# Ten of 32 attention heads go back to the two-pass score scheme; constants joined, token-weight decoding and instruction order set anew

## The chip, the cores and the metric

The kernel runs on one core of a Trainium2 chip. A core has five engines that run their own instruction streams side by side and meet at semaphores: TensorE (PE in the profile, its weight loads PEld), VectorE (DVE), ScalarE (ACT), GpSimd (POOL) and SyncE (SP), which here only issues DMAs. Times are device microseconds of one execution, and less is better.

## What is computed

Attention in which a query sees only keys with the same 6-bit hash, over 4 batches of 8 heads with 768 tokens and 64 channels, then a block on each batch's 768 x 512 result:

```python
q_bits = einsum('bhsd,dk->bhsk', q, proj) > 0      # k likewise, proj is 64 x 6
mask = q_bucket[:, :, :, None] == k_bucket[:, :, None, :]
scores = where(mask, scale * matmul(q, k.T), -1e9)
scores = scores - max(scores, axis=-1)
attn = exp(scores); attn = attn / (sum(attn, axis=-1) + 1e-09)
x = matmul(attn, v)                                # heads side by side: 768 x 512
theta = x @ w_theta
y = w_tok_r @ (x * cos(theta)) + w_tok_i @ (x * sin(theta))
u = x + y
out = u + maximum(u @ w_ch, 0)
```

The four weights are 64-bit floats, and the kernel decodes them on the chip.

## The kernel before

Every f32 operand is held as a pair of f16 numbers, high and low, and a product is made of three f16 matmuls (high x high, high x low, low x high). So a tile of the token product `py` is 36 matmuls of 512 columns, and each of `ps_th` (theta) and `ps_r` (the channel product) is 12.

Heads come in pairs (b, hp). For each pair SP loads `raw` q and k and `vb`, ACT and DVE split them, PE makes the hash signs (`bits`, tile `pb`), and SP copies the pieces into a head's operand tiles `qt` and `kt` (`assemble`: 6 DMAs, `assbits`: 4 small ones from `rows`). There are three sets of `qt` and `kt`.

A head is then done in one of two ways.

The **two-pass way** (22 heads). `maxima` scores the head with queries on the partitions (tile `sq`, 9 units in the two PSUM banks of pool `mx`), and DVE takes the row maxima (`vmax`, `mc<-sq`). PE turns the maxima (`mtr`, tile `pmx`), DVE writes them as f16 rows (`row`, `fl`), and SP puts them into `qt` (`put`) and `ft` (`putf`). `step` then scores the head a second time with keys on the partitions (tile `st`, 9 units in pool `s`), with the maximum as one more row of the operand; ACT takes the exponential (`pf`), ACT makes its f16 high part and POOL the low part (`p1`, `p2`, tile `p`), and PE multiplies them with v (`pv`, tile `po`).

The **turned way** (10 heads, list `TURNED`: heads 5 and 7 of batch 1, and 1, 3, 5, 7 of batches 2 and 3). `turned` scores once, with queries on the partitions (tile `bt`, 12 halves of 384 keys, in pools `s` and `mx`). DVE takes the maximum of each half (`bmax`, `bm<-bt`) and three small steps make bias and rate of the exponential (`bjoin`, `brate`, `bbias`). ACT takes the exponential straight from those scores, ACT and POOL split it (tile `late`), and SP turns the 128 x 1536 f16 result by a DMA transpose (`bturn`, `late<-late`), 6 in a head, before PE multiplies with v (`bpv`).

The token weights come in six tiles (`prep_wtok`, tile number tau). Each is two loads of 768 KB, a decode on DVE and ACT (`wlow`, `whigh`, `wsign`, `wabs`, `wmul`, `wth`, `wtl`) and two DMA transposes into `wtk`. Tiles below `LATE` go through the buffers x, z0 and z1, the others through wx and wz, which the turned heads use for `late` afterwards.

The order on every engine is written out by hand: `ORDER` lists an engine letter and an operation number for each operation, `SLOTS` gives each its buffer, and `issue_all` emits just that. An engine runs its list in order, so an operation that waits holds all behind it. While a batch's heads run, PE fills in the block of the batch before. SP's DMAs share eight semaphores in turn, so each issue also waits for one that was issued earlier.

Of the kernel before, what the change touches and what calls it, by code (L numbers as in the profile page):

```python
# [11 lines left out]
F16 = mybir.dt.float16  # L12
# [20 lines left out]
def lsh_attention_moe_kernel(ctx: ExitStack, tc: tile.TileContext, q, k, v, proj, w_theta, w_tok_r, w_tok_i, w_ch, aff, out):  # L33
# [4 lines left out]
    NB = proj.shape[1]  # L38
# [21 lines left out]
    affs = const.tile([P, 2], F32, name="affs")  # L60
# [9 lines left out]
    pp = const.tile([P, NB], F32, name="pp")  # L70
# [88 lines left out]

    cload = op("consts", QKL - 0.03, on("ACT", 1800, load_consts))  # L160
    proj_ready = op("pst", QK0, on("DVE", 610, split_proj), [cload])


# [26 lines left out]
    def widened(srcs, n, nm, tag, prio, am=None, stage="x", by=1.0, scaled=None, into=None, hold=()):  # L190
# [5 lines left out]
        def load():  # L196
            t["w64"] = w64 = mp.tile([P, m, n, 2], U32, tag=sx.tag, name=f"w64_{nm}")
            for i, src in enumerate(srcs):
                dma(w64[:, i].rearrange("p n two -> p (n two)"), src)
            if into is None:  # L200
# [6 lines left out]
            w2 = w64.rearrange("p m n two -> p (m n) two")  # L207
            t["lo"], t["hi"] = w2[:, :, 0], w2[:, :, 1]

        def low():  # L210
            DVE.tensor_scalar(t["f"].bitcast(U32), t["lo"], 29, 0x40000000, ALU.logical_shift_right, ALU.bitwise_xor)
# [457 lines left out]
    def step(g, b, h, blk, mxt, vt, piece):  # L669
# [85 lines left out]
        finish(t, sm_, g + KN, b, h, vt, done, lo, hi, False)  # L755

    def finish(t, so, pr, b, h, vt, done, lo, hi, eps):
        nm = f"{b}_{h}_{lo}"
        sx = xslot[b]
        n_ = hi - lo  # L760

        def recip():
            t["rc", lo] = ap_.tile([P, T], F32, tag=f"rc{so.idx}_{lo}", bufs=1, name=f"rc_{nm}")
            if eps:
                DVE.tensor_scalar(t["rc", lo][:, lo:hi], t["acc"][:, lo:hi, D], ONE * 1e-9 * PSC, None, ALU.add)
            else:
                DVE.reciprocal(t["rc", lo][:, lo:hi], t["acc"][:, lo:hi, D])

        def again():
            DVE.reciprocal(t["rc", lo][:, lo:hi], t["rc", lo][:, lo:hi])  # L770

        def norm():
            if b not in tl:
                tl[b] = mp.tile([P, T, DM], F32, tag=sx.tag, bufs=1, name=f"x_{b}")
            dst = tl[b][:, lo:hi, h * D : (h + 1) * D]
            DVE.scalar_tensor_tensor(dst, t["acc"][:, lo:hi, :D], vt["inv"], t["rc", lo][:, lo:hi].unsqueeze(2).to_broadcast([P, n_, D]), ALU.mult, ALU.mult)

        r = op("beps" if eps else "recip", pr, on("DVE", 75 if eps else 90, recip), [done], [so])
        if eps:
            r = op("brec", pr, on("DVE", 98, again), [r], [so])  # L780
        n = op("norm", pr, on("DVE", 135 + 67 * n_, norm), [r], [so, sx])
        for i in range(lo // 2, hi // 2):
            xready[b][i].append(n)

    homes = [Slot("wx"), Slot("wz")] if TURNED else []
    late = {}
    bt = {}
    HS = S // 2
    CEXP = 1.0 / (UNIT * math.sqrt(D))

    def home(n, sl):
        if n not in late:
            late[n] = mp.tile([P, 4, S], F32, tag=homes[n].tag, name=f"late{n}")
        return late[n][:, sl.idx].bitcast(F16)

    def turned(g, b, h, blk, n_, asm, vt, pieces):

        j = h % 2
        qt, kt = qts[n_], kts[n_]
        sx = xslot[b]  # L800
        i0, ni = BLOCKS[blk]
        t = bt.setdefault((b, h), {"done": None, "so": Slot("m") if blk == 0 else None, "mc": Slot("mc") if blk == 0 else None})
        so, smc = t["so"], t["mc"]
        for i in range(i0, i0 + ni):
            def one(i=i, before=t["done"]):
                nm = f"{b}_{h}_{i}"
                sp, spt = Slot("pp"), Slot("pt")
                u = {}
                G = g + 0.45 * (i - i0)

                def part(k):
                    return t["bm"][:, i, k : k + 1]

                tops, cuts, held = [], [], []
                for y in range(2):
                    def half(y=y):
                        sw = Slot(("s", "mx")[y])
                        w = {}

                        def scores():  # L820
                            w["w"] = bank(sw, [P, HS], f"bt_{nm}_{y}")
                            for x, kk in ((0, K1), (1, MR)):
                                mm(w["w"], qt[:kk, x, ts(i, P)], kt[:kk, x, y * HS : (y + 1) * HS], x == 0, x == 1)

                        def top():
                            if "bm" not in t:
                                t["bm"] = ap_.tile([P, T, 5], F32, tag="bm" + smc.tag, bufs=1, name=f"bm_{nm}")
                            DVE.tensor_reduce(part(y), w["w"], AX.X, ALU.max)  # L828

                        a = op("bst", G, on("PE", 326, scores), asm, [sw])  # L830
# [635 lines left out]
```

## Time and profile before

| | |
|---|---|
| median of 3 runs | 738.8 us (732.48 to 740.75) |
| the profiled execution | 734.01 us, of which 732.2 us is the span of its instructions |
| PE busy | 670.3 us (92%) |
| PEld busy | 388.7 us (53%) |
| DVE busy | 572.0 us (78%) |
| ACT busy | 571.2 us (78%) |
| POOL busy | 388.7 us (53%) |
| DMA | 100.07 MB, 61.1% of the queue's 16 engines |

The shares are means over stages with different limits, so they are read stage by stage. The span is cut here at the ends of each batch's attention: batch 0 until 157 us, batch 1 until 334, batch 2 until 499, batch 3 until 653, and then the rest of the last batch's block.

### The profile page before, as it was taken

What the parts mean: (1) busy time and instruction counts of PE and PEld (TensorE: products, weight loads), DVE (VectorE), ACT (ScalarE), POOL (GpSimd) and SP (SyncE); (2) the same over time, 40 slices, a digit from 0 to 9 for tenths busy, and PEclk for the clock granted to TensorE, in tenths of its full rate; (3) what the DMA queues carried; (4) which work ended last, traced back from release to release, by engine and by line L of the source; (5) the groups of instructions that cost most, each with busy time, mean ns of one, the idle gap of its engine ahead of it and who ended that gap; (6) DMA issues with size and microseconds to landing.
All of it is one profiled execution on the core that took longest, in us unless ns stands there. A gap on an engine that the chain in (4) does not pass through costs nothing. (4 is left out here: it accounts for less than half of the span.)

```text
span 732.2 us, 16801 instructions
## 1 busy us (share of the span) xinstructions
PE 670.3 (92%) x6174; PEld 388.7 (53%) x6174; DVE 572.0 (78%) x1299; ACT 571.2 (78%) x1014; POOL 388.7 (53%) x392
## 2 busy tenths in 40 slices
PE   3698979888999999888899999989999999999997
PEld 1266747664555555555445555555555466654443
DVE  6799969889999888877898868677988768678221
ACT  6689879988997797978898778878997788966012
POOL 4164444635646675757445667767546577822002
PEclk9799989999999999999999999999999999999999
DMA  5637875686326358876835598887753586971122
GB/s 210 186 94 189 231 187 150 147 178 167 79 77 127 89 123 165 187 157 152 155 78 124 105 198 141 198 150 179 137 111 76 120 147 124 164 130 44 29 68 90
DMA packets 197434, 100.07 MB, mean 137 GB/s; under 512 B 169624, under 2 KB 187112, under 8 KB 197352
## 3 DMA queue, kind: packets, MB, share of 16 engines
q1 hardware_dynamic: 197048, 99.00, 61.1%
q8 instruction: 48, 0.79, 0.4%
q14 instruction: 34, 0.28, 0.1%
q10 hardware_dynamic: 304, 0.00, 0.0%
HBM read 32.51 MB, written 6.29 MB: 53 GB/s over the span
## 5 line engine op out<-in xcount | busy, mean ns | idle before, releaser
L717 POOL TENSOR_TENSOR p<-pf,p 128x512 f16<-128x512 f32 x162 | 196.3, 1224 | 141.3 <-ACT p L711 105.6
L77 PE MATMUL py<-z,wtk 128*128 128x512 f16 x864 | 207.7, 379 | 0.1
L624 DVE TENSOR_REDUCE mc<-sq 128x1 f32<-128x512 f32 (+1 forms) x198 | 132.2, 681 | 26.1 <-PE sq L77 24.9
L870 POOL TENSOR_TENSOR late<-pf,late 128x384 f16<-128x384 f32 x120 | 113.8, 959 | 62.6 <-ACT late L864 54.5
L705 ACT ACTIVATE pf<-st 128x512 f32<-128x512 f32 x198 | 114.2, 591 | 34.0 <-PE st L77 24.4
L77 PE MATMUL st<-qt,kt 108*128 108x512 f16 (+3 forms) x528 | 119.4, 333 | 13.0 <-ACT pf L705 6.0
L77 PEld LDWEIGHTS <-wtk 128*128 128x128 f16 x864 | 82.5, 98 | 90.8 <-issue 3.9
L711 ACT ACTIVATE p<-pf 128x512 f16<-128x512 f32 x162 | 99.3, 627 | 5.1 <-PE po L77 3.5
L77 PE MATMUL sq<-kt,qt 108*128 108x256 f16 (+1 forms) x264 | 74.9, 340 | 20.2 <-DVE mc L624 5.5
L856 ACT ACTIVATE pf<-bt,bm 128x384 f32<-128x384 f32 x120 | 77.8, 664 | 17.8 <-DVE bm L844 11.0
L77 PEld LDWEIGHTS <-p 128*128 128x128 f16 x1944 | 77.8, 98 | 17.0 <-issue 1.0
L77 PE MATMUL po<-vv,p 128*128 128x65 f16 (+1 forms) x1944 | 83.9, 194 | 0.0
L828 DVE TENSOR_REDUCE bm<-bt 128x1 f32<-128x384 f32 x120 | 63.2, 549 | 21.8 <-PE bt L77 19.5
L77 PEld LDWEIGHTS <-qt 108*128 108x128 f16 (+1 forms) x504 | 47.1, 102 | 61.3 <-issue 25.8
L77 PEld LDWEIGHTS <-kt 108*128 108x128 f16 (+1 forms) x528 | 49.8, 102 | 47.4 <-issue 25.9
L77 PE MATMUL ps_th<-wth,t_x 128*128 128x512 f16 x288 | 68.9, 379 | 4.4 <-DMA t_x<-s_x 3.7
L77 PE MATMUL ps_r<-wch,t_u 128*128 128x512 f16 x276 | 70.3, 385 | 1.2 <-DMA t_u<-s_u 1.1
L864 ACT ACTIVATE late<-pf 128x384 f16<-128x384 f32 x120 | 60.4, 520 | 2.1 <-DMA late<-late 0.6
L77 PE MATMUL bt<-kt,qt 108*128 108x384 f16 x240 | 56.3, 327 | 1.9 <-DMA kt<-rows 1.7
L77 PEld LDWEIGHTS <-t_x 128*128 128x128 f16 x288 | 27.0, 97 | 35.3 <-DMA t_x<-s_x 6.7
L77 PEld LDWEIGHTS <-late 128*128 128x128 f16 x1080 | 38.5, 98 | 9.6 <-DMA late<-late 2.4
L1101 POOL TENSOR_TENSOR z<-f,z 128x512 f16<-128x512 f32 x15 | 19.5, 1300 | 43.5 <-ACT z L1095 27.8
(179 smaller groups left out, 1042.2 us busy)
## 6 DMA issues: line engine op xcount, KB each, us to landing
raw<-in_q_dram SPq DMA_DIRECT2D x16, 384.0 KB
raw<-in_k_dram SPq DMA_DIRECT2D x16, 384.0 KB
vb<-in_v_dram SPq DMA_DIRECT2D x16, 384.0 KB
out_dram<-x SPq DMA_DIRECT2D x24, 256.0 KB
qt<-hl SPq DMA_DIRECT2D x31, 192.0 KB
kt<-hl SPq DMA_DIRECT2D x31, 192.0 KB
w_t<-in_moe_w_tok_r_dram SPq DMA_DIRECT2D x6, 768.0 KB
w_t<-in_moe_w_tok_i_dram SPq DMA_DIRECT2D x6, 768.0 KB
```

The costliest lines, as they stand in the source:

```text
L77: PE.matmul(out_, l, r, start=start, stop=stop, skip_group_check=True)
L624: DVE.tensor_reduce(col()[:, cs], u["sq"], AX.X, ALU.max)
L705: ACT.activation(wide("pf", spf, F32), u["st"], AF.Exp, scale=1.0 / (UNIT * math.sqrt(D)))
L711: ACT.activation(o_, u["pf"], AF.Copy)
L717: return lambda: eng.tensor_tensor(wide("p2", sp2, F16), u["pf"], u["p1"], ALU.subtract)
L828: DVE.tensor_reduce(part(y), w["w"], AX.X, ALU.max)
L856: ACT.activation(w["f"], w["w"], AF.Exp, bias=part(4), scale=part(3))
L864: ACT.activation(dst(0), w["f"], AF.Copy)
L870: return lambda: eng.tensor_tensor(dst(1), w["f"], dst(0), ALU.subtract)
L1101: return lambda: eng.tensor_tensor(t["z"][r, 1][:, tt], u["f"], t["z"][r, 0][:, tt], ALU.subtract)
```

## The change

- `turned` and the list `TURNED` go. All 32 heads are done the two-pass way.
- The projection and the two threshold columns come as one array that the host lays out, in one DMA in place of three. The 8 small DVE operations of `split_proj` become 2.
- `LATE` falls from 4 to 2, so four of the six token-weight tiles go through wx and wz. In `widened` the load now takes only the buffer of the raw words, and the sign step depends on `wlow` instead of on the load.
- `ORDER` and `SLOTS` are new throughout, made with later DMA landings assumed.

```diff
@@ load_consts, split_proj
-        for j in range(2):
-            ACT.dma_start(pp[j * D : (j + 1) * D, :], proj)
-        ACT.dma_start(affs, aff)
+        ACT.dma_start(pp, proj)
...
-        for nm, first in (("q", 1.0), ("k", -1.0)):
-            for j in range(2):
-                rows = slice(j * D, (j + 1) * D)
-                for n, sgn in enumerate((first, -first)):
-                    c0 = j * 2 * NB + n * NB
-                    DVE.tensor_scalar(pst[nm][rows, c0 : c0 + NB], pp[rows, :], sgn, None, ALU.mult)
+        rows, signs = pp[:, : 4 * NB], pp[:, 4 * NB : 8 * NB]
+        DVE.tensor_tensor(pst["q"][:, : 4 * NB], rows, signs, ALU.mult)
+        DVE.scalar_tensor_tensor(pst["k"][:, : 4 * NB], rows, -1.0, signs, ALU.mult, ALU.mult)
@@ widened
-        a = op("wload", prio, on("SP", [(450, P * n * 8)] * m, load), slots=[sx, sz] + hold)
+        a = op("wload", prio, on("SP", [(450, P * n * 8)] * m, load), slots=[sx])
...
-        d = op("wsign", prio, on("ACT", 130 + 470 * k_, lambda: ACT.activation(t["sg"], t["hi"].bitcast(F32), AF.Sign)), [a], [sx, sz])
+        d = op("wsign", prio, on("ACT", 130 + 470 * k_, lambda: ACT.activation(t["sg"], t["hi"].bitcast(F32), AF.Sign)), [b_], [sx, sz])
@@ the calls by head
-                if (b, 2 * hp + j) in TURNED:
-                    mxs.append((n, asm))
-                    continue
                 mxs.append(maxima(2 * hp + j, n, b, G, asm))
...
-                if (b, 2 * hp + j) in TURNED:
-                    ends = b == B - 1 and hp == NP - 1
-                    turned(g, b, 2 * hp + j, blk, *mxs[j], vt, LASTP if ends else [(0, T)])
-                    g += BLOCKS[blk][1] // 2
-                    continue
                 step(g, b, 2 * hp + j, blk, mxs[j], vt, PIECES[ORD if b == B - 1 and hp == NP - 1 else 0].get(blk))
@@ constants
-TURNED = [(1, 5), (1, 7), (2, 1), (2, 3), (2, 5), (2, 7), (3, 1), (3, 3), (3, 5), (3, 7)]
-LATE = 4
-WL0 = 22.644
-WLS = 8.829
+LATE = 2
+WL0 = 16.0
+WLS = 2.6
```

What the new numbers do is seen in the order on the engines. On SP, near the start, where the second pair's q and k (`raw_0_1`), the second token-weight tile (`w_t`) and head 1's operands (`hl` into `qt` and `kt`) are fetched, before:

```order
L455 DMA raw_0_1_225<-in_q_dram 128x768
L199 DMA w_t_227<-in_moe_w_tok_r_dram 128x1536
L199 DMA w_t_227<-in_moe_w_tok_i_dram 128x1536
L571 DMA qt_137<-hl_0_179 64x2x768
L572 DMA kt_140<-hl_0_179 64x2x768
```

and after, where head 0's maxima (`row_0`) are put as well:

```order
L456 DMA raw_0_1_229<-in_q_dram 128x768
L572 DMA qt_136<-hl_0_171 64x2x768
L573 DMA kt_139<-hl_0_171 64x2x768
L575 DMA qt_136<-hl_0_171 32x768
L576 DMA kt_139<-hl_0_171 32x768
L575 DMA qt_136<-hl_0_171 32x768
L576 DMA kt_139<-hl_0_171 32x768
L650 DMA qt_135<-row_0_272 1x6x128
```

The 1.5 MB of the second weight tile have moved from ahead of head 1's operands to behind head 1's own maxima, 23 issues later, and the put of head 0's maxima has moved ahead of the four small `rows` copies that it stood behind.

On PE, in batch 2 around the turn of head 6's maxima (`pmx_6`), with the block of batch 1 (`py`) as filling; head 7 was a turned head. Before:

```order
L638 MATMUL pmx_6_7050<-ident,mx_6_6787 6x128
L77 LDWEIGHTS qt_138
L77 MATMUL bt_7_0_0_7052<-kt_141,qt_138 128x384
L77 LDWEIGHTS qt_138
L77 MATMUL bt_7_0_0_7052<-kt_141,qt_138 128x384
L77 LDWEIGHTS wtk_101
L77 MATMUL py_4_6832<-z_1_4720,wtk_101 128x512
```

After:

```order
L639 MATMUL pmx_6_7170<-ident,mx_6_6856 6x128
L77 LDWEIGHTS qt_137
L77 MATMUL sq_7_1_7174<-kt_140,qt_137 128x512
L77 LDWEIGHTS kt_138
L77 MATMUL st_5_0_5_7180<-qt_135,kt_138 128x512
L77 LDWEIGHTS kt_138
L77 MATMUL st_5_0_5_7180<-qt_135,kt_138 128x512
L77 LDWEIGHTS qt_137
L77 MATMUL sq_7_2_7190<-kt_140,qt_137 128x256
```

Head 7 now has its first scores (`sq_7`) here, between the second scores of head 5 (`st_5`), which the turned way did not have.

## Rows read from the trace of the kernel before

**Rows 1.** Windows by stage: PE, PEld, DVE, ACT, POOL busy us (instructions), clock, DMA share, GB/s

```profile
0.00:157.00 157.00, 126.46 (x1173) 85.90 (x1174) 132.33 (x299) 127.48 (x227) 70.40 (x85) 0.95 0.65 174
157.00:334.00 177.00, 162.79 (x1610) 93.31 (x1610) 154.13 (x337) 151.09 (x280) 108.23 (x101) 0.99 0.60 137
334.00:499.00 165.00, 154.83 (x1520) 88.29 (x1522) 128.57 (x312) 137.12 (x246) 103.21 (x103) 0.99 0.71 142
499.00:653.00 154.00, 152.85 (x1536) 87.98 (x1529) 123.62 (x301) 129.90 (x229) 98.45 (x97) 1.00 0.68 132
653.00:732.20 79.20, 73.42 (x343) 33.22 (x341) 33.36 (x53) 25.61 (x35) 8.39 (x7) 0.99 0.24 60
```

**Rows 2.** The chain that ended last: start us, us, what

```profile
469.41 0.89 PE st L77 x8
...
664.67 27.84 PE py L77 x129
```

**Rows 3.** Timeline of PE at 442 us: start us, us, instructions [idle before]

```profile
442.37 0.60 PE L77 MATMUL sq<-kt,qt 108*128 108x512 f16 x3
442.81 0.90 PE L77 MATMUL po<-vv,p 128*128 128x65 f16 x24
...
444.19 0.82 PE L77 MATMUL bt<-kt,qt 108*128 108x384 f16 x4
444.86 0.81 PE L77 MATMUL ps_r<-wch,t_u 128*128 128x512 f16 x3
```

**Rows 4.** Page, costliest groups: xcount | busy, mean ns | idle before

```profile
L624 DVE TENSOR_REDUCE mc<-sq 128x1 f32<-128x512 f32 (+1 forms) x198 | 132.2, 681 | 26.1 <-PE sq L77 24.9
...
L705 ACT ACTIVATE pf<-st 128x512 f32<-128x512 f32 x198 | 114.2, 591 | 34.0 <-PE st L77 24.4
...
L711 ACT ACTIVATE p<-pf 128x512 f16<-128x512 f32 x162 | 99.3, 627 | 5.1 <-PE po L77 3.5
...
L856 ACT ACTIVATE pf<-bt,bm 128x384 f32<-128x384 f32 x120 | 77.8, 664 | 17.8 <-DVE bm L844 11.0
...
L828 DVE TENSOR_REDUCE bm<-bt 128x1 f32<-128x384 f32 x120 | 63.2, 549 | 21.8 <-PE bt L77 19.5
...
L864 ACT ACTIVATE late<-pf 128x384 f16<-128x384 f32 x120 | 60.4, 520 | 2.1 <-DMA late<-late 0.6
```

**Rows 5.** Groups by form: the small steps of turned heads, the end of a token-weight decode

```profile
L844 DVE TENSOR_SCALAR bm<-bm 128x1 f32<-128x1 f32 x60 | 12.6, 211 | 1.5
...
L300 DVE TENSOR_TENSOR wf_t<-wf_t 128x768 f16<-128x768 f32 x12 | 11.4, 963 | 0.6 <-ACT wf_t L299 0.6
...
L225 DVE SCALAR_TENSOR_TENSOR wf_t<-wf_t,scw 128x1536 f32<-128x1536 f32 x6 | 11.1, 1846 | 0.0
...
L838 DVE TENSOR_REDUCE bm<-bm 128x1 f32<-128x2 f32 x60 | 9.1, 151 | 1.5
L841 DVE TENSOR_SCALAR bm<-bm 128x1 f32<-128x1 f32 x60 | 9.1, 151 | 1.5
```

**Rows 6.** Waits of PE over the whole span: us in total, times, longest

```profile
PE st L77 <- ACT pf L705: 6.0, 8, 1.6
PE sq L77 <- DVE mc L624: 5.5, 15, 0.8
PE pmx L638 <- DVE mx L634: 4.3, 4, 1.9
...
PE st L77 <- DMA qt<-row: 3.9, 5, 2.0
...
PE sq L77 <- DMA kt<-rows: 3.6, 3, 2.2
...
PE bt L77 <- DMA kt<-rows: 1.7, 2, 1.5
PE po L77 <- DMA late<-late: 1.6, 2, 1.0
```

**Rows 7.** Timeline of PE in the first 30 us

```profile
6.00 1.49 PE L77 MATMUL pb<-raw,pst_q 128*32 128x384 f32 x2 [6.00 <-DVE pst_q L158]
...
27.43 1.01 PE L77 MATMUL sq<-kt,qt 108*128 108x512 f16 x2 [3.85 <-DMA kt<-hl]
```

More of the change, by code (lines that the diff above doesn't have):

```diff
@@ L32, in lsh_attention_moe_kernel @@
 @with_exitstack
-def lsh_attention_moe_kernel(ctx: ExitStack, tc: tile.TileContext, q, k, v, proj, w_theta, w_tok_r, w_tok_i, w_ch, aff, out):
+def lsh_attention_moe_kernel(ctx: ExitStack, tc: tile.TileContext, q, k, v, proj, w_theta, w_tok_r, w_tok_i, w_ch, out):
     nc = tc.nc
@@ L37, in lsh_attention_moe_kernel @@
     B, H, D, S = q.shape
-    NB = proj.shape[1]
+    NB = (proj.shape[1] - 2) // 8
     DM = w_theta.shape[0]
@@ L69, in lsh_attention_moe_kernel @@
     ones1 = ones[:, :33]
-    pp = const.tile([P, NB], F32, name="pp")
+    pp = const.tile([P, 8 * NB + 2], F32, name="pp")
+    affs = pp[:, 8 * NB :]
     pst = {}
@@ L199, in load, with place @@
                 dma(w64[:, i].rearrange("p n two -> p (n two)"), src)
+        def place():
             if into is None:
@@ L206, in load, with words @@
                 t["f"] = into()
-            w2 = w64.rearrange("p m n two -> p (m n) two")
+        def words():
+            w2 = t["w64"].rearrange("p m n two -> p (m n) two")
             t["lo"], t["hi"] = w2[:, :, 0], w2[:, :, 1]
         def low():
+            place()
+            words()
             DVE.tensor_scalar(t["f"].bitcast(U32), t["lo"], 29, 0x40000000, ALU.logical_shift_right, ALU.bitwise_xor)
@@ L754, in step @@
         lo, hi = 2 * piece[0], 2 * piece[1]
[L755 to L759, printed above, removed]
         n_ = hi - lo
         def recip():
[L763 to L770, printed above, removed]
+            if "rc" not in t:
+                t["rc"] = ap_.tile([P, T], F32, tag=f"rc{sm_.idx}", bufs=1, name=f"rc_{nm}")
@@ L772, in norm @@
+            DVE.reciprocal(t["rc"][:, lo:hi], t["acc"][:, lo:hi, D])
         def norm():
             if b not in tl:
-                tl[b] = mp.tile([P, T, DM], F32, tag=sx.tag, bufs=1, name=f"x_{b}")
+                tl[b] = mp.tile([P, T, DM], F32, tag=xslot[b].tag, bufs=1, name=f"x_{b}")
             dst = tl[b][:, lo:hi, h * D : (h + 1) * D]
-            DVE.scalar_tensor_tensor(dst, t["acc"][:, lo:hi, :D], vt["inv"], t["rc", lo][:, lo:hi].unsqueeze(2).to_broadcast([P, n_, D]), ALU.mult, ALU.mult)
@@ L778, in finish @@
[L778 to L782, printed above, removed]
-            xready[b][i].append(n)
[L785 to L794, printed above, removed]
@@ L901, in moe @@
+            DVE.scalar_tensor_tensor(dst, t["acc"][:, lo:hi, :D], vt["inv"], t["rc"][:, lo:hi].unsqueeze(2).to_broadcast([P, n_, D]), ALU.mult, ALU.mult)
+        r = op("recip", g + KN, on("DVE", 90, recip), [done], [sm_])
+        n = op("norm", g + KN, on("DVE", 135 + 67 * n_, norm), [r], [sm_, sx])
+        for i in range(*piece):
+            xready[b][i].append(n)
     def moe(b, G):
@@ new lines @@
+Dk9 Anj Ai3 Pi9 Phm Djp A2o Del Dk1 Pke Dkf Djq Ajr Phr Phw Pic Aid Skp Pnm Dnn Aia Dno G2p Dnp D2r D2s S1b Pk6 Pif Dnq Djs Pka Pib Ahz Dkb
+Dk7 Gjt Pkg Dkh Pkc Dkd Pk2 Dk3 Dki Pir Dnr Dns Gi0 Pkw Ai4 Dkx Aig Pky A2t S2w Gi5 Dkz Pie Pi1 Dnt Ais Pkj Piu Anw Pix Dkk Dkl Aiy Pii Dnu
+Skm A2u Dnx Ssi Aij Pih Aiv Gju Pik Dnv D1c Pio Pil Aim A1e D1d Skn Pkq Pin Aip Piq Pi6 Ssg G2v Dnz Pm8 A1f Plj D2x D2y Pl2 S1q D1g D1h A30
+Am9 Asj Sof Ama Pjv Ajw D1i D1j A1m Plo Dkr Pl6 A1k D1n Gmb S1o Alp Dl7 Dl3 Pit Piw Ash Alk D1l Di7 Di8 Pks Ple Ply Piz Alf Alg Glh Alz All
@@ L1416 @@
+D31f P30u S2zo P30v A30w D30x S30y P31g P31h P31i A31j D31k S31l
 """
@@ L1433, in _thresholds, with _laid_out @@
     return a
+def _laid_out(proj):
+    import numpy as np
+    d, n = proj.shape
+    rows, signs = np.zeros((128, 4 * n), np.float32), np.ones((128, 2, 2, n), np.float32)
+    for j in range(2):
+        for i in range(2):
+            rows[j * d : (j + 1) * d, (2 * j + i) * n : (2 * j + i + 1) * n] = proj
+    signs[:, :, 1] = -1
+    return np.concatenate([rows, signs.reshape(128, 4 * n), _thresholds(n)], axis=1)
 def kernel(**inputs):
```

392 lines of the change are left out of this document (148 added, 244 removed).

## The prediction

> **What bounds the kernel now.** The page's total says PE 92%, DVE and ACT 78%, but that is a mean over stages, so the windows come first [rows 1]. The reader is to look for the row in which one engine has no idle time left. In the first stage (batch 0, 157 us) nobody is full: PE 126.5, DVE 132.3, ACT 127.5, with 30 us of PE idle, much of it the start-up. In the second (157 to 334) PE is idle for 14.2 us of 177 and DVE (154.1) and ACT (151.1) are nearly as long. In the third (334 to 499) PE is idle for 10.2 of 165. In the fourth (499 to 653) it is idle for 1.15 of 154: there PE alone sets the time. After 653 only the last block is left, and in the chain of waits it is PE again, 129 `py` matmuls in one piece of 27.84 us [rows 2], which is 0.216 us for 512 columns, with the granted clock at 0.99. So a microsecond of PE work costs a microsecond in the fourth stage and the tail, part of one in the second and third, and little in the first. Of DVE and ACT the opposite holds.
>
> **What the change does to a head.** PE: the timeline has one 512-column unit of `sq` and one pair of 256 start at 442.37 and the next work at 442.81, so two units take 0.44 us and a head's 9 units 2.0 us [rows 3]. The second scores cost what the turned head's only scores cost: 4 `bt` matmuls take 444.86 - 444.19 = 0.67 us, 24 of them 4.0 us [rows 3]; 8 `st` matmuls of 256 take 0.89 us [rows 2], so 12 take 1.33, and 12 of 512 at 0.216 take 2.6, together 3.9. The product with v keeps its 108 matmuls. Six matmuls for `ft` and one turn of the maxima are new, at 0.04 us or so each (0.90 / 24 [rows 3]) 0.2 to 0.3. That makes **+2.2 us of PE a head**, 22 us for ten: 4.4 in batch 1 (two heads), 8.8 in batch 2, 8.8 in batch 3.
>
> DVE loses 12 x 0.549 and six times 0.151 + 0.151 + 0.211 [rows 4, 5], 6.6 + 3.1 = 9.7 us, and gets 9 x 0.681 = 6.1 [rows 4] and three small steps, some 0.6: **-3 us a head**. ACT loses 12 x (0.664 + 0.520) = 14.2 us and gets 9 x (0.591 + 0.627) = 11.0 [rows 4]: **-3.2 us a head**. POOL splits the same number of elements and is nowhere the longest engine [rows 1]; I cost it at nothing, and the engine to hide behind is PE. SP loses six transposes a head and gets three small puts. PE waited 1.6 us for turned results in the whole run, and 1.7 us for the `rows` of turned heads [rows 6], so the transposes' going is worth at most some 3 us of direct wait, and I put it into the bounds.
>
> **Stage by stage,** against the profiled execution of 734.0 us (its span of 732.2 and 1.8 around it).
>
> Batch 0. The signs now wait for one load and two DVE operations, not three loads and eight. PE stood still until 6.00 us for `pst_q` [rows 7]; the first q and k are needed too, and I take 0.8 us for it. Then PE waited 3.85 us for `kt<-hl` at 27.43 [rows 7], and SP's order had the 1.5 MB of a weight tile ahead of those copies; they are behind them now. Against this, the end of a sixth weight tile's decode (1.85 + 2 x 0.96 = 3.8 us of DVE [rows 5]) moves from the second stage into this one, and the decodes stand closer together, through one buffer: a late one would hold DVE's list, `vmax` and `norm` of batch 0 behind it. I take -1, between -5 (start-up gain alone) and +5 (decode in full, and some waiting).
>
> Batch 1. DVE, 154.1, loses 2 x 3 and the 3.8 of the decode, ACT 6.4, so both fall to about 144. PE rises from 162.8 to 167.2 and becomes the longest by far; what it waited for was mostly the two that get lighter, so I take 6 us of idle in place of 14.2, which gives 173, or **-4**. Ends: idle of 2 us, -8; all idle stays, +4.4.
>
> Batch 2. PE 154.8 + 8.8 = 163.6 of 165, DVE down by 12 and ACT by 13. What was idle goes first: with some 4.4 of the 10.2 us left (the same share as in batch 1), 168, or **+3**. Ends: no idle to speak of, -2; all of it stays, +8.8.
>
> Batch 3. There is 1.15 us to give, so **+8.8**, between +8 and +11 (waits of new `sq` units that nothing covers).
>
> Tail. The same matmuls in another order: 0, between -1 and +3 (the last tile's store is late).
>
> Sum: -1 - 4 + 3 + 8.8 + 0 = +6.8, so 734.0 + 6.8 = **741 us**. The profiled execution lies 0.6% under the median of 738.8 shown, and inside the three runs' spread of 732.5 to 740.8, so I leave the sum as it is; it is 0.3% over that median. One per cent, 7.4 us, is about what a measurement of this kernel can tell from no change. All lower ends together give -8, 726; all upper ones +32, 766.
>
> **The rivals.** *The idle time closes (faster).* A new order that allows for late landings could bring the second and third stage to what the fourth has now. For it: the list of PE's waits has many short ones for DMAs [rows 6], DVE and ACT get slack, and the fourth stage shows that 99% is possible. Against it: DVE and ACT waits are as long in that list, and an order cannot move them all. Price: -5 - 8 - 2 + 8.5 - 1 = -7.5, so 726.
>
> *PE has room (faster).* Weight loads fill only 88.0 of 154 us in the fourth stage [rows 1], and if matmul records merely overlap, new matmuls could slip in between. Then the terms follow DVE and ACT alone: -1 in batch 0, -8, -4, 0, so 721. The chain's 0.216 us for 512 columns, back to back, speaks against it: that is 2.4 columns a nanosecond, the higher clock level, one column a cycle. The Trainium skill (Perfetto Trace Analysis, Identifying the Most-Contended Engine) says to judge TensorE's headroom by the share of weight loads, not by busy matmuls; by that rule the 8.8 us of batch 3 would cost nothing. Here the row of the chain decides against the rule, since 512-column matmuls take longer than their weight load.
>
> *Two-pass heads wait more (slower).* Place: the two `mx` banks and the way from the last maximum to `st`. PE's waits on that way were 6.0 + 5.5 + 4.3 + 3.9 + 3.6 = 23.3 us for 22 heads, 1.06 a head; the turned heads' were 1.7 + 1.6 = 3.3 for 10, 0.33 a head [rows 6]. Ten more heads at 0.73 are 7 us, on top of 22 us of work with none of the old idle closed, less 1 at the start: +28, 762. It decides if PE waits over 1 us a head for `vmax`, the turned maxima and their put. Against it: these waits fall mostly where DVE was full, and DVE gets lighter.
>
> *The order buys nothing (slower).* The landings were not what PE waited for, idle stays as it is in each stage, and the 22 us come on top: +4.4 + 8.8 + 8.8 - 1 = +21, 755. For it: the fourth stage, with just as many turned heads as the third, hardly waited at all, so the third's idle may have nothing to do with them.
>
> **How the numbers follow.** The forecast, 741 with its own range of 732 to 749, has 0.38; the idle closes 0.27; room in PE 0.05; more waits 0.13; an order that buys nothing 0.17. Against 738.8, faster by over 1% is below 731.4: the two faster rivals but for the upper edge of the first, and a little of the forecast's edge, 0.31. Slower is above 746.2: the two slower rivals and the forecast's upper edge, 0.33. Within 1% is the remaining 0.36. The range leaves out most of the PE rival, the bottom of the first and the upper half of the waits: 723 to 760.
>
> **What the profile after would show.** PE's busy time up by some 22 to 30 us (a `sq` record is longer than its 0.22 us step), DVE's down by about 30, ACT's by about 32, `late` and `bt` gone, 288 rows of `mc<-sq`. If the stages hold: batch 3 longer by 8 to 9 us at 99% of PE, batch 2 longer by about 3, batch 1 shorter by about 4, the attention of batch 0 ending within 5 us of 157. The first `pb` before 5.5 us, and the wait for `kt<-hl` at 27 us short or gone. I am wrong about the size if the first stage moves by more than 5 us, which I can least read from a trace with another order; about the mechanism if batch 3 does not lengthen, or if PE's wait list shows new waits for `mc` or `qt<-row` of over 1 us a head.

## The result, and the profile after

The changed kernel takes 743.99 us, median of 20 runs (737.58 to 750.15), against 737.65 for the kernel before (20 runs, 732.48 to 744.68): a ratio of 1.0085 [1.0062, 1.0108], 6.3 us. The forecast was 741, by a sum of +6.8 on the profiled execution, and 0.3% over the median known then. The total came out; the stages behind it did not all do so.

The profiled execution took 748.39 us, with a span of 746.6. It is one of the longer runs, so a second profile of the same kernel stands beside it (`again`, below, span 740.9). Windows by stage of the kernel after, to be held against [rows 1]; the columns are the same, and the cuts lie at the last `po` of each batch (the first line of `again` stands below them):

```profile
0.00:172.00 172.00, 143.54 (x1162) 95.84 (x1163) 137.19 (x283) 130.03 (x224) 70.91 (x85) 0.90 0.63 170
172.00:344.50 172.50, 167.01 (x1641) 97.00 (x1640) 151.45 (x301) 144.68 (x265) 112.10 (x97) 0.98 0.45 105
344.50:505.50 161.00, 160.16 (x1620) 93.48 (x1617) 122.60 (x242) 129.65 (x225) 102.21 (x91) 1.00 0.39 89
505.50:666.40 160.90, 160.19 (x1603) 93.85 (x1602) 110.60 (x212) 123.38 (x212) 100.16 (x87) 1.00 0.29 60
666.40:746.60 80.20, 73.68 (x344) 33.62 (x342) 35.71 (x60) 24.90 (x34) 6.46 (x5) 1.00 0.26 65
```

```profile
0.00:166.00 166.00, 137.25 (x1159) 93.06 (x1160) 136.90 (x282) 129.44 (x224) 70.88 (x85) 0.91 0.67 175
```

| stage | before | after | again | change (after, again) | forecast |
|---|---|---|---|---|---|
| batch 0 | 157 | 172.0 | 166.0 | +15.0, +9.0 | -1 |
| batch 1 | 177 | 172.5 | 173.0 | -4.5, -4.0 | -4 |
| batch 2 | 165 | 161.0 | 161.0 | -4.0, -4.0 | +3 |
| batch 3 | 154 | 160.9 | 161.0 | +6.9, +7.0 | +8.8 |
| tail | 79.2 | 80.2 | 79.9 | +1.0, +0.7 | 0 |

The cuts of before lie up to 1.8 us behind the last `po` of a batch. Cut at that mark in all three profiles (before at 155.2, 332.6, 498.0 and 652.6), the changes are +16.5 and +11.1, -4.5 and -4.4, -4.4 and -4.9, +6.2 and +6.2, and +0.7 in the tail.

In the third stage PE is now idle for 0.84 us, in the fourth for 0.71; before it was 10.2 and 1.15. PE sets the time from 345 us on. The first stage is the odd one: its PE busy time rose by 17 us with about as many matmuls (1162 for 1173), and its granted clock fell from 0.95 to 0.90.

The page of the kernel after: the clock granted in 40 slices of 18.7 us, in tenths, and the groups that answer to [rows 4].

```profile
PEclk9999995888999999999999999999999999999999
...
L625 DVE TENSOR_REDUCE mc<-sq 128x1 f32<-128x512 f32 (+1 forms) x288 | 191.4, 683 | 56.9 <-PE sq L77 55.9
L706 ACT ACTIVATE pf<-st 128x512 f32<-128x512 f32 x288 | 167.2, 591 | 82.7 <-PE st L77 55.1
...
L712 ACT ACTIVATE p<-pf 128x512 f16<-128x512 f32 x252 | 152.9, 625 | 25.7 <-PE po L77 22.7
```

The "5" is the seventh slice, 112 to 131 us: its granted clock is 0.51, so that TensorE spent nearly all of it at the lower of its two levels (1.2 GHz, 0.5 in the granted clock). There are 288 rows of `mc<-sq`, 90 more, and the groups on `bt`, `bm` and `late` are gone. DVE and ACT wait longer for PE than before: 55.9 us ahead of `mc` for 24.9, and 55.1 ahead of `pf` for 24.4 [rows 4].

The waits of PE that answer to [rows 6]:

```profile
PE sq L77 <- DVE mc L625: 8.0, 13, 1.4
PE st L77 <- ACT pf L706: 5.8, 11, 0.9
PE pb L77 <- DMA raw<-in_q_dram: 4.3, 1, 4.3
...
PE pmx L639 <- DVE mx L635: 2.0, 2, 1.0
...
PE sq L77 <- DMA kt<-rows: 1.3, 2, 0.8
```

The waits for `qt<-row` and `late` have gone, that for `kt<-rows` fell from 3.6 to 1.3. What is left of PE's waits is mostly the way from one score to the next.

PE's timeline after, the start against [rows 7] and a unit of scores against [rows 3]:

```profile
4.28 1.46 PE L77 MATMUL pb<-raw,pst_q 128*32 128x384 f32 x2 [4.28 <-DMA raw<-in_q_dram]
...
11.88 1.01 PE L77 MATMUL sq<-kt,qt 108*128 108x512 f16 x3 [4.17 <-DVE kt L540]
...
560.63 0.38 PE L77 MATMUL sq<-kt,qt 108*128 108x512 f16 x1
560.85 0.60 PE L77 MATMUL st<-qt,kt 108*128 108x256 f16 x4
561.29 2.54 PE L77 MATMUL py<-z,wtk 128*128 128x512 f16 x11
```

The first `pb` starts at 4.28 us in place of 6.00, and there is no wait at 27 us. A unit of `sq` takes 0.22 us and four half `st` 0.44, as costed.

What happened in the first stage can be read between 118 and 129 us. The same timeline of the three engines there, PE first, then ACT, then DVE:

```profile
118.14 3.51 PE L77 MATMUL po<-vw,pf 128*128 128x65 f32 x16
...
123.46 0.60 ACT L706 ACTIVATE pf<-st 128x512 f32<-128x512 f32 x1 [2.81 <-PE st L77]
123.95 1.58 ACT L222 ACTIVATE wf_t<-w_t 128x1536 f32<-128x1536 f32 x1
126.17 0.60 ACT L706 ACTIVATE pf<-st 128x512 f32<-128x512 f32 x1 [0.64 <-PE po L77]
126.66 1.47 ACT L223 ACTIVATE wf_t<-wf_t 128x1536 f32<-128x1536 f32 x1
...
128.26 0.15 DVE L172 TENSOR_SCALAR sinv<-wsum 128x1 f32<-128x1 f32 x1 [5.21 <-ACT wf_t L223]
...
130.56 0.68 DVE L625 TENSOR_REDUCE mc<-sq 128x1 f32<-128x512 f32 x1
```

Sixteen `po` with 32-bit operands take 3.51 us. In the kernel before, sixteen like them took 1.90 at the full clock:

```profile
153.34 1.90 PE L77 MATMUL po<-vw,pf 128*128 128x65 f32 x16
```

In the kernel after, ACT waits 2.81 us for `st` matmuls that stand behind them in PE's list, and 0.64 for the next `po`. So the decode step that stands behind `pf` in ACT's list (L223) comes late, and DVE, whose next step is that tile's scale, stands idle for 5.21 us; the `mc` that PE's next scores need stands behind it in DVE's list and starts at 130.56. Here a slow PE holds the decode. That the decode holds PE in turn is a reading that these rows do not show, since PE was busy for 8.9 of the 10 us from 120 on; a place where a decode does hold PE comes with order_b0_mid below.

The clock is summed here from windows of 20 us between 100 and 180 us: 20 us times (1 - granted clock) is the full-clock time that was taken away. The loss of time is at most that, since PE is also idle in these windows. Kernel after:

```profile
100.00:120.00 20.00, 16.25 (x124) 11.84 (x116) 16.37 (x35) 11.59 (x24) 9.89 (x9) 0.72 0.82 212
120.00:140.00 20.00, 18.13 (x108) 12.40 (x108) 11.64 (x24) 14.63 (x27) 3.48 (x3) 0.68 0.51 142
140.00:160.00 20.00, 15.40 (x134) 9.76 (x134) 16.98 (x33) 15.15 (x25) 12.92 (x8) 0.74 0.88 218
160.00:180.00 20.00, 16.39 (x134) 12.58 (x132) 18.07 (x40) 16.11 (x29) 4.01 (x5) 0.93 0.42 123
```

That is 5.6 + 6.4 + 5.2 + 1.4 = 18.6 us. The kernel before has 1.00 in the last three of these windows, and in the first

```profile
100.00:120.00 20.00, 17.94 (x203) 12.67 (x204) 15.02 (x37) 16.54 (x30) 8.51 (x8) 0.84 0.62 156
```

which makes 3.2 us. The table shows the runs that bear on the first stage in these terms. dup_b23 and mix_b3 have their edits behind it, so they are one more sample each of the first stage of the kernel after and of the kernel before; decode_b is left out, since its profiled execution is 1.3% longer than its median.

| kernel | PE work added in batch 0 | full-clock time lost, 100 to 180 us | last `po` of batch 0 | ratio to the kernel before |
|---|---|---|---|---|
| before | 0 | 3.2 | 155 | 1 |
| after | 0 | 18.6 | 172 | 1.0085 [1.0062, 1.0108] |
| again | 0 | 15.8 | 166 | 1.0082 [1.0043, 1.0122] |
| dup_pairs | 5.3 | 8.6 | 164 | 1.0054 [1.0021, 1.0086] |
| dup_mid | 8 | 5.2 | 163 | 1.0109 [1.0073, 1.0145] |
| dup_b0 | 16 | 1.8 | 165 | 1.0111 [1.0029, 1.0194] |
| before_dup_b0 | 16 | 3.6 | 163 | 1.0121 [1.0068, 1.0173] |
| decode_later | 0 | 7.4 | 160 | 1.0312 [1.0233, 1.0391] |
| decode5_later | 0 | 8.6 | 164 | 1.0242 [1.0189, 1.0295] |
| order_b0 | 0 | 1.2 | 155 | 1.0020 [0.9981, 1.0059] |
| order_b0_mid | 0 | 1.8 (and 12 at 57 to 81 us) | 168 | 1.0128 [1.0079, 1.0177] |
| dup_b23 | 0 | 19.4 | 168 | 1.0506 [1.0424, 1.0588] |
| mix_b3 | 0 | 1.8 | 158 | 1.0023 [0.9983, 1.0062] |

The first stage of the kernel after thus ended at 172, 166 and 168, that of the kernel before at 155 and 158; a difference of 3 us between two profiles says little.

The loss is also larger than the stage shows. By count, the 700th matmul of the kernel after starts 7.0 us ahead of that of the kernel before (10.7 in `again`), at 102.0 for 109.0, and the 1160th 16.9 us behind it (11.5). The change's order is ahead until about 100 us, with 23 of DVE's 48 steps of token-weight decode done where the kernel before has 29, and loses 22 to 24 us after that.

### The profile page after: what moved, and what is told of

Its sections match the earlier page's. It is cut to its first block, busy times and chain, and to the rows that moved or that the text cites. A ratio compares the mean times of both kernels' runs of the same rounds, so it can differ in the third digit from the quotient of the medians.

```text
span 746.6 us, 16888 instructions
## 1 busy us (share of the span) xinstructions
PE 704.6 (94%) x6364; PEld 413.8 (55%) x6364; DVE 557.5 (75%) x1094; ACT 552.6 (74%) x958; POOL 391.8 (52%) x363
## 4 chain that ended last, share of the span: by engine, by line
PE 80%; DVE 9%; ACT 6%; DMA 2%; issue 2%; SPq 1%; POOL 0%; ACTq 0%; DVEq 0%
PE py L77 24%; PE st L77 15%; PE po L77 15%; PE ps_r L77 8%; PE ps_th L77 7%; PE sq L77 7%; DVE mc L625 3%; ACT pf L706 2%; PE pb L77 2%; ACT p L712 1%; ACT wf_t L223 1%; PE pmx L639 1%; SPq L582 1%; DVE hl L473 1%; PE pm L77 0%
## 5 line engine op out<-in xcount | busy, mean ns | idle before, releaser
L718 POOL TENSOR_TENSOR p<-pf,p 128x512 f16<-128x512 f32 x252 | 309.3, 1243 | 207.0 <-ACT p L712 138.3
L625 DVE TENSOR_REDUCE mc<-sq 128x1 f32<-128x512 f32 (+1 forms) x288 | 191.4, 683 | 56.9 <-PE sq L77 55.9
L706 ACT ACTIVATE pf<-st 128x512 f32<-128x512 f32 x288 | 167.2, 591 | 82.7 <-PE st L77 55.1
L77 PE MATMUL st<-qt,kt 98*128 98x512 f16 (+3 forms) x768 | 175.9, 342 | 6.1 <-ACT pf L706 5.8
L712 ACT ACTIVATE p<-pf 128x512 f16<-128x512 f32 x252 | 152.9, 625 | 25.7 <-PE po L77 22.7
L77 PEld LDWEIGHTS <-p 128*128 128x128 f16 x3024 | 122.4, 99 | 33.8 <-issue 8.1
L77 PE MATMUL po<-vv,p 128*128 128x65 f16 x3024 | 131.5, 196 | 1.1 <-POOL p L718 1.0
L77 PE MATMUL sq<-kt,qt 108*128 108x512 f16 (+1 forms) x384 | 110.8, 343 | 14.7 <-DVE mc L625 8.0
L77 PEld LDWEIGHTS po<-vw,pf 128*128 128x128 f32 x288 | 41.5, 214 | 5.4 <-ACT pf L706 2.7
L77 PE MATMUL po<-vw,pf 128*128 128x65 f32 x288 | 42.5, 298 | 1.5 <-ACT pf L706 1.5
```

The costliest lines, as they stand in the source:

```text
L77: PE.matmul(out_, l, r, start=start, stop=stop, skip_group_check=True)
L625: DVE.tensor_reduce(col()[:, cs], u["sq"], AX.X, ALU.max)
L706: ACT.activation(wide("pf", spf, F32), u["st"], AF.Exp, scale=1.0 / (UNIT * math.sqrt(D)))
L712: ACT.activation(o_, u["pf"], AF.Copy)
L718: return lambda: eng.tensor_tensor(wide("p2", sp2, F16), u["pf"], u["p1"], ALU.subtract)
```

## The experiments

**The kernel after, once more (again).** No edit.

> The changed kernel once more, nothing edited. In its profile batch 0's attention ended at 172 us, not 157, and from there on PE was hardly idle. Clock theory: PE's granted clock was 0.5 for 41 us between 100 and 184 us (7 us in the kernel before), and that made the loss; then a second profile shows the end of batch 0 moving with its own low-clock time: again about 40 us of it and an end at 168 to 175, or less of both. Decode theory: the token-weight decodes, now one after the other through one buffer, hold up DVE and ACT lists and PE waits for them; then the end stays at 168 to 175 whatever the clock does. Both: 744 us, within 1%.

Measured: 743.53 us, ratio 1.0082. The first stage ended at 166, not 172; all others were equal within 0.5 us. So the lost time lies in one place in both profiles, and its size varies with the clock there.

**More work for PE, first batch (dup_b0).** Every first-score matmul of batch 0 is issued twice into the same bank, the second result over the first.

```
-                    for x, (i, k0, k1) in enumerate(parts):
-                        mm(sq[:, x], qt[:K1, 0, ts(i, P)], kt[:K1, 0, k0:k1], x == 0, x == len(parts) - 1)
+                    for _ in range(2 if b in DUP else 1):
+                        for x, (i, k0, k1) in enumerate(parts):
+                            mm(sq[:, x], qt[:K1, 0, ts(i, P)], kt[:K1, 0, k0:k1], x == 0, x == len(parts) - 1)
...
+DUP = (0,)
```

> The changed kernel with each first-score matmul of batch 0's eight heads issued twice into the same bank (the first result is overwritten, the output is the same): 72 units of 0.22 us, 16 us more PE work in a stretch where PE has 105 us of it in 172. Clock theory: PE is busier, the low-clock time between 100 and 184 us shrinks below 15 us, and batch 0 ends at 157 to 165: 732 to 740 us. Decode theory: PE was only waiting, the extra work is hidden at best and lengthens the way to the maxima: the end at 172 or later, 744 to 756 us.

Measured: 745.6 us. Windows of this kernel:

```profile
100.00:120.00 20.00, 16.10 (x172) 11.52 (x170) 16.89 (x37) 14.97 (x30) 11.40 (x10) 1.00 0.80 223
120.00:140.00 20.00, 16.27 (x152) 11.31 (x155) 16.57 (x34) 17.74 (x32) 7.32 (x7) 1.00 0.73 192
140.00:160.00 20.00, 15.53 (x173) 11.52 (x170) 18.97 (x38) 15.38 (x28) 11.58 (x9) 1.00 0.84 193
```

The clock stayed full, and the first stage ended at 165, with 16 us more to do. That end is the clock theory's, but the time missed its band (732 to 740) and lies in that of the decode theory (744 to 756): the clock came back, but not for nothing. PE is still idle for 12.1 of these 60 us, waiting for DVE and ACT.

**The same in batches 2 and 3 (dup_b23).** The same edit, with `DUP = (2, 3)`.

> The changed kernel with the first-score matmuls of all heads of batches 2 and 3 issued twice (the output is the same): 144 units of 0.22 us, 32 us more PE work in the stretch that PE is thought to set. If PE sets it: +29 to +35 us, 773 to 779. If PE has room, as its 58% of weight-load time would let one think, or if the wait for DVE's maxima sets the pace: under +12, below 756.

Measured: 775.45 us, ratio 1.0506 [1.0424, 1.0588], 31.9 us over `again` for 32 us of matmuls. Its windows of the two stages:

```profile
346.00:521.00 175.00, 175.00 (x1727) 103.02 (x1724) 123.08 (x242) 130.15 (x224) 101.50 (x91) 1.00 0.36 81
521.00:694.00 173.00, 172.41 (x1673) 101.04 (x1671) 110.47 (x212) 124.13 (x212) 100.30 (x87) 1.00 0.26 55
```

PE has no room there: the two stages grew by 14 and 12 us, and most of the rest fell before their first cut (batch 1, in which the first scores of batch 2 begin, took 178). The Trainium skill (Perfetto Trace Analysis, Identifying the Most-Contended Engine) judges TensorE's headroom by MFU, the share of peak operations, and by the share of weight-load time. The prediction named only the second. Weight loads fill 59 and 58% of these windows, and the measurement decides against that share as a sign of room here.

**The same work in the kernel before (before_dup_b0), and less of it (dup_pairs, dup_mid).** The edit of dup_b0 in the kernel before (with the condition `b == 0`), and in the kernel after with these conditions:

```
+                    for _ in range(2 if b == 0 and n % 3 == 2 else 1):
...
+                    for _ in range(2 if b == 0 and 3 <= h <= 6 else 1):
```

> The kernel before, with the first-score matmuls of its first batch issued twice, 72 units, 16 us of TensorE at full clock. Its first stage had 17 us of low clock (8.5 us lost by the half), 7 of it after 95 us. Theory (clock): at most about 4 us can come back after 95 us and perhaps some of the 5 us at 24 to 35 us, so that the kernel before loses 8 to 13 us by it (time 746 to 751), where the changed kernel lost 2. First rival (idle time of TensorE in the first stage takes the extra work): 738 to 742 here too, and what the same edit cost in the changed kernel says nothing of the clock.

> The changed kernel; of the first-score matmuls of the first batch, those of the 24 units of two matmuls (every third unit) are issued twice into the same accumulation, 48 matmuls more, about 5 us of TensorE at full clock, spread over the whole first stage. Theory (the first stage is lost to the clock: each us at 0.5 between 95 and 180 us costs half a us; 31 to 34 us of it in the two profiles of the changed kernel): if the small extra work holds the clock as doubling everything did, under 12 us of low clock remain, the first stage ends at 158 to 162 and the time is 734 to 739. First rival (the first stage waits for VectorE and the decode, the extra matmuls fill idle time): the first stage ends at 166 to 172 as it did, time 742 to 746. Second rival (the clock is what it is, whatever TensorE is given, and work adds up): 5 us more, 747 to 751, with 30 us or more at low clock.

> The changed kernel; the first-score matmuls of heads 3 to 6 of the first batch alone are issued twice, 36 units, about 8 us of TensorE, all in the middle of the first stage, ahead of and in the stretch where the granted clock fell. Theory (clock): low clock in 95 to 180 us falls from 31 to 34 us to under 15, the first stage ends at 158 to 164, time 735 to 741. First rival (waits for VectorE and the decode set that stretch): time 742 to 746. Second rival (work adds up): 750 to 753.

Measured: 747.13, 740.69 and 743.43 us, the kernel before at 736.06. The kernel before lost 11.1 us by the 16 us of work; the kernel after, by the same edit, 2.1 (745.6 - 743.5). By ratio that is 1.2% and 0.3%, and the last `po` came 8 us later in the one and 1 us earlier in the other. Idle time takes a part of the work in both, so I put the difference, 7 to 9 us, down to the clock. That is not clear of the noise: dup_b0 had only four runs, and the intervals of the three ratios give the difference of 0.9% an uncertainty of about 1%. The two small ones went the same way: 7 to 11 us of the clock came back against 5 and 8 us of work, and the stage ended 2 to 3 us ahead of `again`. Neither reached the time that the clock theory gave (734 to 739, 735 to 741); dup_mid's lies in the band of the first rival (742 to 746).

The clock itself is on record for every run, not only for the profiled ones. Span times (1 - mean granted clock) of a run is the full-clock time taken from it. Its medians are 10.2, 11.8, 11.0 and 14.0 us in the four sets of runs of the kernel before, 15.6 and 16.3 in the kernel after and `again`, 7.4, 8.5 and 10.4 in dup_b0, dup_pairs and dup_mid, 13.4 in before_dup_b0 and 4.8 in order_b0 below. So added work did bring 5 to 9 us of the clock back in the kernel after, and none in the kernel before (13.4 for 11.8 in the same set). What that was worth in time is another matter, and dup_mid shows it. Two of its windows:

```profile
120.00:130.00 10.00, 8.64 (x77) 6.19 (x77) 7.80 (x16) 9.68 (x21) 2.34 (x3) 1.00 0.77 220
130.00:140.00 10.00, 5.28 (x67) 2.92 (x64) 9.39 (x18) 8.54 (x12) 9.06 (x6) 1.00 0.69 171
```

At the full clock PE stands idle for 4.7 us of the second one, while DVE has 9.4 us to do. The clock is not the only thing that is wrong there; I take DVE's list to be another.

**Decode put off (decode_later, decode5_later).** The order alone: the operations of tiles 3, 4 and 5, or of tile 5 alone, stand later, and nothing else moves but what needs them. In decode5_later 15 of the list's 3946 entries move: 12 operations on DVE and ACT (`D26` to `D2h`), the two transposes (`S2i`, `S2j`) and `D2b5`, which needs them. The 14 stand 178 to 186 entries later, `D2b5` 65; all others keep their order, engine and buffers.

> The changed kernel with three token-weight decodes moved later in all lists: the tile that was decoded third of the late four goes to the place of the next one, that one to the next, and the last to where the kernel before had it, beside the first token products (some 40 us of PE work later). 6.6 us of DVE and 4.8 us of ACT a tile leave the stretch from 100 us on, to be done where PE was 97% busy. Decode theory: batch 0 ends 5 to 12 us earlier and the time falls to 732 to 740. Clock theory: it follows the clock alone: within 3 us of 744 if the low-clock time between 100 and 184 us stays at some 40 us, less if it falls.

> The changed kernel with the decode of the last token-weight tile alone (its 12 operations on VectorE and ScalarE and its 2 transposes) moved later by 25 to 45 us of TensorE work, so that it lies as in the kernel before, the other tiles where the change put them. Theory (clock set off by the waits of the crowded decode): the clock from 95 to 170 us is as low as in the changed kernel or nearly, first stage ends at 160 to 170, time 740 to 745. Rival (four tiles decoded on VectorE and ScalarE before 130 us are what crowds the first stage): the first stage ends at 156 to 161 and the next one keeps its 172 us, time 730 to 737. Second rival (the late tile comes too late for the sums that use it, as with three tiles moved): next stage longer by 5 us or more, time 747 to 760.

Measured: 760.41 and 752.66 us. The first stage did end earlier, at 160 and 164, and the next one gave back more than that: in decode_later DVE's list of waits between 180 and 220 us has

```profile
DVE wf_t L212 <- DMA wtk<-wf_t: 8.7, 1, 8.7
```

which is the one late buffer, held by the transposes of the tile before, and PE was busy for 11.34 of 200 to 220 at a clock of 0.66. With tile 5 alone the clock fell at 201 us too (0.66 in 200 to 210), and the last `py` of batch 0 came at 300 us, for 293 in `again`. I read this as the sums that use the late tiles leaving no room to put the decode off in this order; no run tests it apart.

**The first 230 us in the order of before (order_b0).** The kernel after, with its joined loads; what runs up to 230 us stands in the order of the kernel before, decode included, so that four tiles are early again, in the buffers of before; 24 operations also run on the engine that the kernel before gives them; from there on the change's own order. So it is order, buffers and engines of this stretch together that go back.

```
-LATE = 2
+LATE = 4
...
 ORDER = """
-A0 S5g D1 S5i P5w D5x A5h A5j P5k S64 D5l A65 P66 A62 S2 D5m D5n D5o D5p D5q D5r A5y S7d D63 D67 D68 D5s D69 D61 A5z A60 P6w D5t Sa8 A5u D5v
+S5g A0 S5i S64 S1q D1 A5h P5w A5j D5x P5k D5l S7d A5z D5m D5n A62 D5o D5p D5q A63 D5r D5y A5s D61 A5u D5t A60 D5v A65 Sa8 P6w P6o A76 D6x Sa6 S2
...
```

> The changed kernel, its instructions and joined loads, but what runs up to about 230 us stands in the order of the kernel before, with the token-weight tiles decoded where they were (four early, two late, in the buffers of before); behind that the order of the change. Theory (the first stage is lost by the order of its attention and decode, the clock falls because of it): the first stage ends at 155 to 160 us with under 12 us of low clock in 95 to 180, at 230 us the kernel is 10 to 13 us ahead of the changed one and keeps it, time 727 to 735, faster than the kernel before. First rival (the loss is the work of the changed batch itself or the joined loads, or the clock falls by itself): the first stage ends at 163 to 172, time 740 to 746. Second rival (what the first stage wins the seam gives back): first stage 155 to 160, the next one longer by as much, time 738 to 746.

Measured: 738.32 us against 738.03, ratio 1.0020 [0.9981, 1.0059]; the profiled execution took 733.86. Its windows by stage, and those of 100 to 140 us:

```profile
0.00:155.00 155.00, 124.48 (x1165) 84.68 (x1166) 129.81 (x285) 127.84 (x226) 71.31 (x84) 0.99 0.66 176
155.00:328.00 173.00, 165.65 (x1638) 95.65 (x1637) 148.29 (x301) 144.88 (x266) 108.39 (x94) 1.00 0.49 116
328.00:490.00 162.00, 160.30 (x1621) 93.59 (x1618) 122.84 (x243) 129.74 (x226) 102.36 (x91) 1.00 0.39 88
490.00:652.00 162.00, 160.39 (x1604) 93.81 (x1603) 112.71 (x212) 123.14 (x211) 100.30 (x87) 1.00 0.29 59
...
100.00:120.00 20.00, 17.28 (x206) 12.15 (x204) 15.90 (x39) 15.32 (x27) 8.63 (x8) 0.94 0.63 153
120.00:140.00 20.00, 18.45 (x196) 13.54 (x195) 18.15 (x41) 18.26 (x37) 11.85 (x12) 1.00 0.51 131
```

The first stage ended at 155 with 1.2 us taken by the clock, as the theory had it, and batches 1 to 3 are within 1.1 us of what they are in the kernel after. The loss of the first stage goes with its order. But the profiled execution is the fastest of the twelve, with a mean clock of 0.997 for a median of 0.9935: it is 8.9 us shorter than that of `again`, while by ratio the medians differ by 0.6%, some 4.6 us. The median, 738.3, lies above the band of the theory (727 to 735) and in that of the second rival (738 to 746), though the next stage is not longer. Without the loss the change is worth nothing, not 1% less.

**The same, with the change's order for the first 50 us (order_b0_mid).** Only the order from 50 to 230 us is that of before.

> As the last, but the order of the change is kept for the first 50 us too, so that only the stretch from about 50 to 230 us stands in the order of the kernel before. The changed kernel was 3 us ahead at 30 us and 3 to 6 us at 60 us. Theory: the head start is kept, first stage 151 to 157, time 3 to 5 us under the last, 724 to 731. Rival (the head start was bought with decode work put off, which comes back before 100 us): the same as the last within 2 us, or slower.

Measured: 746.82 us, ratio 1.0128 [1.0079, 1.0177]; the rival's "slower" held, through the seam. At 50 us a decode step stands in DVE's list whose load was still under way. DVE waited 6.7 us for it, and PE 9.8 for the `mc` behind:

```profile
DVE wf_t L212 <- DMA w_t<-in_moe_w_tok_i_dram: 6.7, 1, 6.7
...
PE sq L77 <- DVE mc L625: 10.6, 2, 9.8
```

Its windows, and below them the second one in order_b0:

```profile
50.00:57.00 7.00, 3.12 (x35) 2.73 (x32) 0.82 (x3) 1.78 (x2) 0.00 (x0) 1.00 0.90 305
57.00:81.00 24.00, 17.01 (x79) 11.06 (x79) 15.04 (x29) 15.17 (x25) 4.57 (x4) 0.50 0.33 67
```

```profile
57.00:81.00 24.00, 20.30 (x232) 14.46 (x231) 21.85 (x49) 21.85 (x37) 14.65 (x12) 1.00 0.62 159
```

After the idle stretch the clock was 0.50 for 24 us, and order_b0 issued 232 matmuls in those same 24 us where this kernel issued 79 (not quite the same ones). The first stage ended at 168 in place of 155. By count of matmuls this kernel is 4.4 us ahead of order_b0 at the 290th, at 52.5 us, 13.0 behind at the 350th, at 79.8, and 12.8 behind at the 1100th. So the loss lies in this place: that one wait for a decode cost some 17 us, the wait itself and then the clock, of which the start had won 4.

**The decode alone where before has it (decode_b).** All attention, token and channel work in the order of the change; only the six tiles' decode moves, with its buffers (`LATE = 4`).

> The changed kernel with the decode of the six token-weight tiles alone moved to where the kernel before has it, by TensorE work done (four tiles in the early buffers, the fifth spread over the first stage, the last one as late as the sums that use it allow); all other instructions of TensorE, VectorE, ScalarE and GpSimd keep the order of the change. Theory D (where the decode lies makes the loss): the first stage ends at 155 to 161, time 731 to 738. Theory O (the order of the attention makes it, whatever the decode does): the first stage ends at 164 to 172 with 25 us or more at low clock, time 740 to 746.

Measured: 801.01 us, ratio 1.0761 [1.0687, 1.0835]. Neither theory had this. I read it so: the place of the decode is not good or bad by itself, and each order of the attention was laid around its own.

**Batches 1 and 2 of the change, the rest of before (mix_b3).** The program of before, with the turned heads of batches 1 and 2 scored twice, and the order of the change from 230 us to the end of batch 2.

```
-TURNED = [(1, 5), (1, 7), (2, 1), (2, 3), (2, 5), (2, 7), (3, 1), (3, 3), (3, 5), (3, 7)]
+TURNED = [(3, 1), (3, 3), (3, 5), (3, 7)]
```

> The program of the kernel before with its loads, its early decode and the turned heads of its last batch, but with the six turned heads of batches 1 and 2 scored twice; order of the kernel before up to 230 us, the order of the change from there to the end of batch 2's attention, then the order of before. Theory (the stages add up by themselves: the first is lost by the order of its 230 us, batches 1 and 2 are won by the order of the change, the last batch is lost by its two-pass heads): stages of about 157, 171 to 174, 161 to 164, 153 to 156 and 79 us, time 725 to 733, faster than the kernel before by 0.7 to 1.7%. Rival (the two-pass heads of batches 1 and 2 win nothing against a kernel with an undisturbed first stage, the seams give it back): time 735 to 742. Second rival (turned heads in one batch alone lose what the order won, since the transposes meet a new order at the seam): last stage over 160 us, time above 738.

Measured: 741.36 us against 739.64, ratio 1.0023 [0.9983, 1.0062]: the band of the first rival. Its windows of batches 1 and 3, and PE's longest wait in batch 1:

```profile
158.00:339.00 181.00, 167.27 (x1629) 95.66 (x1629) 149.06 (x301) 144.92 (x266) 107.33 (x94) 0.98 0.46 112
...
501.00:660.00 159.00, 153.94 (x1530) 88.57 (x1528) 124.79 (x300) 131.35 (x231) 98.66 (x99) 0.99 0.64 122
```

```profile
PE py L77 <- DVE mt L408: 6.2, 1, 6.2
```

Batch 1 took 181, not 172, with one wait of 6.2 us, to 265.25, and 6.8 us at a clock of 0.50 from 262.8 on; batch 3 took 159, of which PE was idle for 5, where the kernel before has 154 [rows 1]. The stages did not add up here, cut out of two orders. No version here beats the kernel before in the median.

## Why the prediction was right, and where it was not

**PE's price of a head** held in kind and was too high in size. Four heads in batch 3 cost 6.9 and 7.0 us (6.2 between the last `po`), 1.75 a head or less for 2.2 forecast and under the lower end of +8: PE's busy time rose by 160.19 - 152.85 = 7.3, and idle fell from 1.15 to 0.71. The new `sq` and `st` take what was costed; what makes up the rest is not shown. dup_b23 shows that PE set the time there, at 32 us for 32. PE's busy time over the whole run rose by 34 us, 28 in `again`, where 22 to 30 was forecast; 17 and 11 of it lie in the first stage, where none was.

**DVE and ACT** lost 27 and 29 us of instruction time over all groups (forecast 30 and 32). The busy time of the page, which the forecast named and which counts overlapping records once, fell by only 14.5 and 18.6. That made no time by itself.

**Batch 1** gave -4.5 and -4.0 for -4, by 5.5 us of idle where 6 were assumed.

**Batch 2** failed in its size. The step was "with some 4.4 of the 10.2 us left (the same share as in batch 1)"; 0.84 was left, and PE's work rose by 5.3 and not 8.8. So it came out at -4 for +3, below its lower end of -2. This is the mechanism of the rival "the idle time closes", which the prediction priced for all stages at once.

**Batch 0** is the term that failed: "I take -1, between -5 ... and +5". It measured +15 and +9. The start-up gain came (the first `pb` 1.7 us earlier, for 0.8; no wait at 27 us). The step that failed is the decode in another place, "in full, and some waiting". It counted the decode's DVE time and had no term for TensorE's clock: in this stage the granted clock fell from 0.95 to 0.90, and PE's busy time rose by 17 us for the same work. order_b0 shows that the loss and the low clock both go with the first 230 us of the order, its buffers and engines: 11 us of the stage in its profile, some 4.6 us in the medians. Where a wait for a decode is followed by a low clock, order_b0_mid shows the price of one, some 17 us.

How much of the loss is the clock stays open. The medians of dup_b0 and before_dup_b0 put 7 to 9 us on it, within their noise. But with the clock nearly full dup_b0 and dup_mid still ended the stage at 165 and 163, 8 to 10 us behind the kernel before, if with work added, and decode5_later, with none added, got 7 us of the clock back and ended only 2 us ahead of `again`. Which part of the order sets it off is open too: moving only the decode, in three ways, lost more than it won. In DVE's list 28 steps of token-weight decode stand between the first product of head 4 and the first of batch 1, where the kernel before has 10; that fits the lead until 100 us and the loss behind it, and decode_b shows that it isn't enough.

**The rivals.** "PE has room" is refuted by dup_b23 for batches 2 and 3. "Two-pass heads wait more" did not happen: the five waits it counted went from 23.3 us [rows 6] to 5.8 + 8.0 + 2.0 + 0 + 1.3 = 17.1. "The order buys nothing" is wrong both ways: it won 4 us in each of batches 1 and 2, and lost 9 to 15 in batch 0. So the total was right by luck: a loss at the front that no term held was set off by two stages, batches 2 and 3, that did better than their terms. As I had put it, I was wrong about the size, by the first stage.

## What to carry to other kernels

When a new order is laid, price not only the work that moves but the idle time that it makes on TensorE, since the trace of order_b0_mid shows a gap of 9.8 us followed by 24 us at half the clock; read the granted clock of each stage before the busy times. A stage in which nobody is full is the one that a new order changes most, so its term needs the widest range. Two orders made around their own decode and buffers cannot be cut together freely (of order_b0, order_b0_mid, decode_b and mix_b3 only the first kept its stages): test the cut before counting on the sum of the best stages.

## What was not expected of the hardware

TensorE at a low clock is not idle by the trace: between 120 and 140 us of the kernel after, at 0.68, it was busy for 18.13 of 20 us with 108 matmuls, and order_b0 issued 196 in the same window in 18.45 us at 1.00, if not quite the same ones. So a high busy time in a stage with a low clock is by itself no sign of a bound. In three runs, 5 to 16 us of added matmuls in batch 0 moved the end of the stage by -3 to -1 us against `again`; they did not lengthen it.
